# The high and low parts of a Strassen stage's results, queued one unit of products later

## The chip, the cores and the metric

The kernel runs on one core of one Trainium2 chip. A time is device microseconds (us) of one execution of the whole program. A core has four engines that matter here, each of which works through its own queue in the order in which the program issued the instructions: TensorE (PE in the profile, its weight loads PEld), VectorE (DVE), ScalarE (ACT) and GpSimd (POOL, which here mostly issues DMAs). An instruction waits at the head of its queue for what it needs from other engines, and everything behind it waits with it.

## The reference, cut to what matters

One block of a network on x of 2048 rows by 512 columns: a Fourier mixing sublayer, then a gated feed-forward sublayer, each behind a layer norm that is modulated from c. The change touches the second sublayer alone:

```python
gate = jnp.einsum("bsd,df->bsf", x, w1)      # 512 -> 1792
up = jnp.einsum("bsd,df->bsf", x, w3)
h = _silu(gate) * up
out = jnp.einsum("bsf,fd->bsd", h, w2)       # 1792 -> 512
```

## The kernel before, in words

**Numbers in two parts.** TensorE multiplies float32 numbers here as two rounded parts: the high part is a rounded copy (made on ACT, `copy`, line 87), the low part is what the copy left over (made on DVE, `minus`, line 90). `product` (line 100 issues its matmuls) is three matmuls: high by high, high of the left operand by low of the right one, low by high. So a result h that is to be multiplied by w2 needs a tile `hf` with a high and a low half, and the second matmul of its product already reads the low half.

**Tiles.** All large tiles are slots of one pool of 50, taken with `take` from the front of a queue of free slots and put back at its end with `give`. PSUM has eight banks; results leave a bank by a copy on ACT or an addition on DVE.

**Groups.** The 1792 columns of w1 and w3 are 7 groups of 256, and the rows are 4 blocks of 512, two pairs of blocks. From about 318 us on, each item, that is one group with one pair of blocks, is done as a Strassen product: 7 products for w1 (named a1 to a7 below) and 7 for w3 (b1 to b7), where plain blocks need 8. There are 12 items (two groups of the first pair are done as plain blocks before): five of the first pair of blocks (items 0 to 4), then seven of the second (items 5 to 11). Of these, items 5 to 9 (`SEVEN`) also take seven products by w2, and the other items take eight plain ones. A product by w2 is written y; it is read out of its bank on ACT (line 335, tile `y`) and added to DRAM by a DMA that GpSimd issues (line 1160 or 1352).

**Units and queues.** One a, b or y is a unit of six matmuls. The order of units is written by hand as strings. For item i, the units before the dash belong to the item before:

```python
body = "a6 a5 y y a7 y a3 y a4 y b1 y b2 y b6 b5 y"
head = "-b7 a1 -b4 -b3 a2 " if i == turning else "-b7 a1 a2 -b4 -b3 " if i else "a1 a2 "
if i == turning:
    body = "y y y y y a6 y a5 y a7 y b1 b2 a4 b6 a3 b5"
```

So four units of an item's w3 products, b7, b4 and b3 among them, run inside the next item, and the first y that uses an item's results comes after its b3: four units after b4 in the stretches of items 1 to 4, and three after b4 in the stretch of item 5 (`turning`), where five y stand in a row. The items of the second pair use shorter bodies, such as "a6 a5 a7 y a3 a4 y b1 b2 y b6 b5 y".

A unit is issued in this sequence: `delayed()` issues whatever an earlier unit put behind itself for now; then the unit's matmuls, and its reading out of the bank; then `beside` lets a planner issue as many waiting jobs (splitting the next weights, the layer norm of the other rows) as the unit's estimated spare time on DVE and ACT pays for. `behind(n, fn)` puts `fn` n units off, to the head of that unit.

**The results.** `factor` runs one a or b. Of the products of w3, b1, b5 and b6 are only copied out (ACT, line 87, tile `x`); b2, b3 and b7 are added to such a copy (DVE, line 93, tile `x`) and b4 is used from its bank. Then `result` (the function of `times`, line 96, tile `v`) multiplies by the silu of the w1 side, and puts two things behind: the high part, `highs` (ACT, line 87, `hf<-v`), and the low part, `lows` (DVE, line 90, `hf<-v,hf`). For the items of `SEVEN` the results go to `seven_parts`, which does the same for b2, b4 and b7 (`high` and `low`) and a row of sums after b3. Results of b2 and b4 feed the first four y of an item, those of b3 and b7 the next four. After b3, the two tiles `v` are given back, also by `behind`.

In b7 the matmuls add to the bank that b6 began with, so b7 can begin only after b6's copy; a7 stands in the same way to a6. A y needs a free bank of two (6 and 7).

## Time and profile before

| what | before |
|---|---|
| median of 3 executions | 696.4 us (695.23 to 697.4) |
| the profiled execution | 694.86 us |
| its span, first to last instruction | 693.1 us |
| granted TensorE clock, mean | 0.997 |
| PE busy | 675.3 us, 3122 matmuls |
| DVE busy | 586.9 us |
| ACT busy | 451.1 us |
| POOL busy | 131.6 us |

Busy time of PE has to be read with care: a matmul record of 128x512 lasts 389 ns, and in an undisturbed run the next one begins 0.23 us after it, so records overlap and short pauses of PE do not show as idle. A pause is seen in the starts: where two matmuls begin further apart than 0.23 us. In the rows of the timeline, the columns are start, duration, engine, line, operation, out<-in, shape, count, and in brackets the idle time before with what ended it. Equal instructions in a row are merged into one row: two merged matmuls that run undisturbed take 0.61 to 0.63 us.

### The profile page before, as it was taken

How to read it: one execution, taken by the hardware profiler on the slowest of the kernel's cores; microseconds unless marked ns; L12 is line 12 of the kernel's file. 1: busy time of each engine (PE TensorE's matmuls, PEld its weight loads, DVE VectorE, ACT ScalarE, POOL GpSimd, SP SyncE). 2: the span in 40 equal slices, each digit the busy share in tenths (PEclk: the TensorE clock that was granted, in tenths of full speed). 3: DMA queues.
4: the chain of work that ended last, by engine and by line, in shares of the span. 5: the costliest groups of instructions: out<-in, count | busy, mean ns of one | idle time of the engine just before them, and what ended most of it. 6: DMA issues, size and time to landing. Idle time of an engine off the chain costs nothing.

```text
span 693.1 us, 9032 instructions
## 1 busy us (share of the span) xinstructions
PE 675.3 (97%) x3122; PEld 558.1 (81%) x3122; DVE 586.9 (85%) x945; ACT 451.1 (65%) x751; POOL 131.6 (19%) x156
## 2 busy tenths in 40 slices
PE   7999899999999999999999999999999999999996
PEld 5899778888888888888788888887877888888785
DVE  5999759998999988889997989787999979888374
ACT  4998946545353575664577767867676988877520
POOL 1320252543435000010101001011002212221100
PEclk9999999999999999999999999999999999999999
DMA  9730289787588540173667666476849898999713
GB/s 264 222 123 1 71 306 352 259 294 253 181 310 263 181 157 30 37 148 122 102 145 147 152 154 117 96 132 121 258 89 208 152 208 168 186 214 172 179 42 126
DMA packets 40261, 116.80 MB, mean 169 GB/s; under 512 B 5136, under 2 KB 5392, under 8 KB 40208
## 3 DMA queue, kind: packets, MB, share of 16 engines
q0 software_dynamic: 14512, 50.86, 36.5%
q1 hardware_dynamic: 25264, 63.98, 27.9%
q10 hardware_dynamic: 432, 1.31, 0.5%
q8 instruction: 26, 0.43, 0.3%
q14 instruction: 27, 0.22, 0.1%
HBM read 76.81 MB, written 41.42 MB: 171 GB/s over the span
## 4 chain that ended last, share of the span: by engine, by line
PE 71%; DVE 9%; issue 7%; DMA 5%; ACT 4%; POOL 1%; SPq 1%; another core or an unknown queue 1%; POOLq 0%; ACTq 0%; DVEq 0%
PE bank L100 43%; PE bank L750 25%; DMA sum<-y 3%; POOL sum L1352 1%; PE bank L559 1%; DMA w<-in_wdr 1%; PE bank L598 1%; ACT y L335 1%; DVE v L96 1%; SPq L231 1%; DMA w<-in_wdi 1%; DVE xr L805 1%; DVE ul L90 1%; DMA x<-in_x 0%
## 5 line engine op out<-in xcount | busy, mean ns | idle before, releaser
L100 PE MATMUL bank<-hf,w2h 128*128 128x512 f32 (+1 forms) x352 | 108.5, 389 | 0.4 <-ACT y L335 0.4
L87 ACT ACTIVATE hf<-v 128x512 fp32r<-128x512 f32 x71 | 44.4, 631 | 69.1 <-DVE v L96 53.7
L335 ACT ACTIVATE y<-bank,gb 128x512 f32<-128x512 f32 x118 | 76.5, 682 | 4.1 <-PE bank L100 3.6
L100 PEld LDWEIGHTS bank<-hf,w2h 128*128 128x128 f32 x352 | 65.5, 188 | 16.1 <-ACT y L335 2.2
L1160 POOL DMA_DIRECT2D sum<-y x28 | 24.0, 857 | 240.7 <-ACT y L335 124.5
L100 PE MATMUL bank<-hf,w2l 128*128 128x512 f32 (+1 forms) x176 | 68.1, 387 | 0.0
L90 DVE TENSOR_TENSOR hf<-v,hf 128x512 fp32r<-128x512 f32 x71 | 48.7, 686 | 9.8 <-ACT hf L87 9.8
L1352 POOL DMA_DIRECT2D sum<-y x35 | 29.8, 852 | 129.4 <-ACT y L335 120.4
L750 PE MATMUL bank<-d,us 128*128 128x512 f32 x128 | 49.9, 390 | 1.5 <-DVE ho L93 1.5
L87 ACT ACTIVATE x<-bank 128x512 f32<-128x512 f32 x72 | 41.7, 591 | 13.3 <-PE bank L100 12.1
L750 PE MATMUL bank<-bh,us 128*128 128x512 f32 x128 | 49.9, 390 | 0.0
L750 PE MATMUL bank<-bh,ul 128*128 128x512 f32 x128 | 49.8, 389 | 0.0
L750 PE MATMUL bank<-d,uh 128*128 128x512 f32 x128 | 49.8, 389 | 0.0
L750 PE MATMUL bank<-l,us 128*128 128x512 f32 x128 | 49.8, 389 | 0.0
L750 PE MATMUL bank<-l,uh 128*128 128x512 f32 x128 | 49.8, 389 | 0.0
L170 POOL DMA_INDIRECT re<-in_ctr,mirror x32 | 35.1, 1095 | 64.8 <-DVE ul L90 38.5
L170 POOL DMA_INDIRECT im<-in_cti,mirror x32 | 32.9, 1029 | 38.2 <-PE bank L750 10.0
L93 DVE TENSOR_TENSOR x<-bank,x 128x512 f32<-128x512 f32 x36 | 24.7, 685 | 17.3 <-PE bank L100 17.1
L100 PEld LDWEIGHTS bank<-hf,w2l 128*128 128x128 f32 x176 | 33.1, 188 | 6.6
L1244 ACT ACTIVATE v<-v 128x512 f32<-128x512 f32 x36 | 22.7, 629 | 22.5 <-DVE v L93 22.1
L93 DVE TENSOR_TENSOR v<-bank,x 128x512 f32<-128x512 f32 x36 | 24.7, 686 | 13.4 <-PE bank L100 12.5
L100 PE MATMUL bank<-h2h,w1h 128*128 128x512 f32 x80 | 31.1, 389 | 0.0
(260 smaller groups left out, 1904.7 us busy)
## 6 DMA issues: line engine op xcount, KB each, us to landing
sum<-y POOLq DMA_DIRECT2D x63, 512.0 KB
w<-in_w SPq DMA_DIRECT2D x42, 512.0 KB
re<-in_ctr SPq DMA_DIRECT2D x32, 256.0 KB
im<-in_cti SPq DMA_DIRECT2D x32, 256.0 KB
wmc<-in_wmc SPq DMA_DIRECT2D x8, 512.0 KB
xr<-in_xt SPq DMA_DIRECT2D x8, 512.0 KB
sum<-xr SPq DMA_DIRECT2D x8, 512.0 KB
x<-in_x SPq DMA_DIRECT2D x11, 256.0 KB
```

The source lines that it names most:

```text
L87: nc.scalar.activation(dst, src, AF.Copy, scale=scale)
L90: nc.vector.tensor_tensor(out=dst, in0=a, in1=b, op=OP.subtract)
L93: nc.vector.tensor_tensor(out=dst, in0=a, in1=b, op=OP.add)
L96: nc.vector.tensor_tensor(out=dst, in0=a, in1=b, op=OP.mult)
L100: nc.tensor.matmul(acc, lhs[a], rhs[b], start=first and n == 0, stop=last and n == len(PASSES) - 1, skip_group_check=more,)
L170: nc.gpsimd.indirect_dma_start(dst, None, rows, bass.IndirectOffsetOnAxis(ap=at, axis=0))
L231: queue.dma_start(raw_w[dt][q * 64 : (q + 1) * 64, m, :], w[i][par::2, q])
L335: nc.scalar.activation(dst, src, AF.Identity, scale=by)
L750: nc.tensor.matmul(acc[what, e], lhs, rhs, start=begin and i == 0, stop=(end or (turn and what == "x")) and i == len(terms) - 1, skip_grou ...
L1160: nc.gpsimd.dma_start(sums[t, d // 2], y, accum_op=OP.add)
L1244: behind(k != 0 or q == 0, lambda: nc.scalar.activation(v, src, AF.Silu))
L1352: nc.gpsimd.dma_start(sums[t, which], y, accum_op=OP.add)
```

## The change

The high part is put two units behind instead of one, the low part three instead of two, for all items and, in the items of `SEVEN`, for b2, b4 and b7. The tiles `v` of the items outside `SEVEN` are given back four units after b3 instead of three. No instruction is added, removed or resized.

```diff
@@ result
-        behind(1, highs)
-        behind(2, lows)
+        behind(2, highs)
+        behind(3, lows)
@@ seven_parts, if (q, k) != (0, 1)
-            behind(1, lambda: high(n, v[q, k]))
-            behind(2, lambda: low(n, v[q, k]))
+            behind(2, lambda: high(n, v[q, k]))
+            behind(3, lambda: low(n, v[q, k]))
@@ factor, n == 3 of w3
-                    behind(9 if items[i] in SEVEN else 3, lambda x=x: give(x))
+                    behind(9 if items[i] in SEVEN else 4, lambda x=x: give(x))
```

## The prediction

> **What bounds the kernel now.** I read the page first, then what PE waits for after 318 us, then the timeline of PE around every place where two matmuls begin further apart than 0.23 us.

> ```profile
> PE 675.3 (97%) x3122; PEld 558.1 (81%) x3122; DVE 586.9 (85%) x945; ACT 451.1 (65%) x751; POOL 131.6 (19%) x156
> L87 ACT ACTIVATE hf<-v 128x512 fp32r<-128x512 f32 x71 | 44.4, 631 | 69.1 <-DVE v L96 53.7 <-issue 6.7 <-DVE v L90 4.7
> ```
> ```profile
> PE bank L100 <- ACT y L335: 0.9, 2, 0.5
> PE bank L100 <- ACT x L87: 0.6, 2, 0.4
> ```

> TensorE is the bound: 97% busy. The copy that makes the high part (71 of them) leaves ACT idle for 69.1 us, of which 53.7 us are for the multiplication on DVE: ACT stands at the head of its queue with nothing to do, and the readings-out of banks wait behind it. But ACT is not the bound, so those 53.7 us are no prize. What they cost is what reaches PE, and the waits of PE name just two engines' work there, both ACT's: y and x. So the question is narrow: which pauses of PE does a late copy make, and which new pauses does the later place make?

> **The change, part by part: what goes.** In item 0's tail, the copy of b2 waits 3.74 us; y, and the copies of b6 and b5 (one row of two) stand behind it, and b7 begins late.

> ```profile
> 342.61 0.63 ACT L87 ACTIVATE hf<-v 128x512 fp32r<-128x512 f32 x1 [3.74 <-DVE v L96]
> ...
> 343.72 1.07 ACT L87 ACTIVATE x<-bank 128x512 f32<-128x512 f32 x2
> ```
> ```profile
> 343.61 0.39 PE L100 MATMUL bank<-hf,w2l 128*128 128x512 f32 x1
> 344.36 0.50 PE L100 MATMUL bank<-th,w3sh 128*128 128x512 f32 x1 [0.36 <-ACT x L87]
> ```
> ```profile
> 374.18 0.39 PE L100 MATMUL bank<-hf,w2l 128*128 128x512 f32 x1
> 374.50 0.50 PE L100 MATMUL bank<-th,w3sh 128*128 128x512 f32 x1
> 374.84 0.40 PE L100 MATMUL bank<-tl,w3sh 128*128 128x512 f32 x1
> ```

> The matmul of b7 begins 0.75 us after the one before it, 0.52 more than 0.23; and a matmul that has waited takes 0.34 until the next (374.50 to 374.84), 0.11 more than usual. So a pause costs its wait plus 0.11, here 0.63. After the change y stands ahead of the copy of b2, which still begins at 342.61; b6's copy then follows at 343.15, 0.57 earlier, and lands at 343.8, when b7 is due at 343.84: the pause goes, **-0.63**. The pause at 374.50 has the same cause and goes: 0.32 - 0.23 + 0.11, **-0.20**.

> In the stretch of item 11, the copies of b7 and b3 do the same to a y, to the next y and to a7:

> ```profile
> 640.63 0.63 ACT L87 ACTIVATE hf<-v 128x512 fp32r<-128x512 f32 x1 [2.15 <-DVE v L96]
> ...
> 642.30 0.59 ACT L87 ACTIVATE x<-bank 128x512 f32<-128x512 f32 x1
> ...
> 649.75 0.63 ACT L87 ACTIVATE hf<-v 128x512 fp32r<-128x512 f32 x1 [2.26 <-DMA sum<-y]
> ```
> ```profile
> 641.39 0.39 PE L100 MATMUL bank<-h2h,w1l 128*128 128x512 f32 x1
> 641.89 0.74 PE L100 MATMUL bank<-hf,w2sh 128*128 128x512 f32 x2
> ...
> 644.55 0.39 PE L100 MATMUL bank<-th,w3l 128*128 128x512 f32 x1
> 644.91 0.74 PE L100 MATMUL bank<-hf,w2h 128*128 128x512 f32 x2
> ```
> ```profile
> 650.30 0.39 PE L100 MATMUL bank<-th,w1sl 128*128 128x512 f32 x1
> 650.92 0.50 PE L100 MATMUL bank<-th,w1sh 128*128 128x512 f32 x1 [0.23 <-ACT x L87]
> ```

> The three pauses are 0.38, 0.24 and 0.50 us by the same sum. A unit later, b7's copy stands behind the two readings of y, and a1's copy comes a good microsecond before 642.30; b3's copy, which waits for a DMA that still reads its slot, stands behind a6's copy instead of ahead of it. All three go: **-1.12**. Together **-1.95**.

> **What comes.** The low part's place is what I count as the loss. The first y of an item reads the low half of b4's result with its fifth matmul, 0.91 us after its start. Before, DVE has it in queue right behind b3's multiplication. Now it is issued one unit later, so it stands behind the jobs of that unit. In the stretch of item 2 these are the four additions `w3s`:

> ```profile
> 383.54 0.69 DVE L96 TENSOR_TENSOR v<-v,x 128x512 f32<-128x512 f32 x1
> 384.15 0.68 DVE L90 TENSOR_TENSOR hf<-v,hf 128x512 fp32r<-128x512 f32 x1
> 384.75 0.42 DVE L93 TENSOR_TENSOR w3s<-w 128x256 f32<-128x256 f32 x1
> ...
> 386.22 0.69 DVE L90 TENSOR_TENSOR hf<-v,hf 128x512 fp32r<-128x512 f32 x1
> ```
> ```profile
> 384.84 0.63 PE L100 MATMUL bank<-hf,w2h 128*128 128x512 f32 x2
> ```

> The low part at 384.15 lands at 384.83; its reader is the second matmul of the pair that begins at 384.84, due at 385.07: only 0.24 us to spare. The four additions take 386.22 - 384.75 = 1.47 us, begin at 384.15 instead, and the low part begins at 385.62 and lands at 386.31. PE waits 1.30 (with the 0.06 from a landing to the start of its reader), plus 0.11: **+1.41**. Nothing hides it: a late low part holds PE, as the pair of 0.84 us in the next rows shows.

> In the stretches of items 3, 4 and 5 the jobs between differ:

> ```profile
> 412.34 0.69 DVE L96 TENSOR_TENSOR v<-v,x 128x512 f32<-128x512 f32 x1
> ...
> 444.94 1.22 DVE L90 TENSOR_TENSOR w3l<-w,w3h 128x1024 fp32r<-128x1024 f32 x1
> ...
> 472.88 1.22 DVE L90 TENSOR_TENSOR tl<-xc,th 128x1024 fp32r<-128x1024 f32 x1
> ```
> ```profile
> 414.82 0.62 PE L100 MATMUL bank<-hf,w2h 128*128 128x512 f32 x2
> ...
> 444.74 0.84 PE L100 MATMUL bank<-hf,w2h 128*128 128x512 f32 x2
> ...
> 472.18 0.73 PE L100 MATMUL bank<-hf,w2h 128*128 128x512 f32 x2
> ```
> ```profile
> 474.52 0.73 PE L100 MATMUL bank<-hf,w2h 128*128 128x512 f32 x2
> ...
> 477.57 0.74 PE L100 MATMUL bank<-hf,w2h 128*128 128x512 f32 x2
> ```

> Stretch of item 3: the multiplication begins at 412.34, the additions 0.61 later, the low part after 1.47 more, at 414.42, and it lands at 415.10; due is the matmul at 414.82 + 0.23. **+0.24** (0.13 and 0.11). Stretch of item 4: here the additions stand ahead already, and the pair takes 0.84 instead of 0.62, so the low part is late today. It falls behind the weights' low part as well, which holds DVE for 1.13 (1.22 less the overlap of two records): **+1.12**. Stretch of item 5, with one unit less between b4 and y: the low part falls behind the addition of a2 (0.60) and a `tl` (1.13), 1.73 later, and is 0.05 late already (0.73 for the pair): +1.78. Three further pairs of this row of y (the first and the last are shown) pause because ACT has a job for each y and falls behind; while PE waits for the low part, ACT catches up, which gives back up to 0.48. I take **+1.30**, with 1.78 and 0.9 as ends. In the stretch of item 1 no job stands in that unit: nothing.

> In the items of `SEVEN`, the copy of b2 filled the time in which DVE made `w2s`, for which the job behind y, the copy `w2sh`, waits. Now that copy stands first and `hf` behind it, ahead of b6's copy:

> ```profile
> 518.75 0.42 DVE L90 TENSOR_TENSOR w2s<-w,w2s 128x256 f32<-128x256 f32 x1
> ```
> ```profile
> 520.36 0.59 ACT L87 ACTIVATE x<-bank 128x512 f32<-128x512 f32 x1
> ...
> 549.71 0.59 ACT L87 ACTIVATE x<-bank 128x512 f32<-128x512 f32 x1
> ```
> ```profile
> 550.47 0.40 PE L100 MATMUL bank<-th,w3sh 128*128 128x512 f32 x1
> ```

> `w2s` is done at 519.17; `w2sh` then holds ACT for 0.95 and `hf` for 0.54, so b6's copy begins at 520.69 instead of 520.36. b7 waits for that copy there today: **+0.33**. An item later the same shift of 0.33 takes b6's copy from 549.71 to 550.04, landing at 550.63 with b7 due at 550.47: 0.22 and 0.11, **+0.33**. Two further items have by the same sum a few hundredths to spare, and I count nothing for them; 0.2 each is the end.

> **The sum:** +1.41 +0.24 +1.12 +1.30 +0.33 +0.33 -1.95 = **+2.8 us** on a span of 693.1, in an execution of 694.86. That execution lies 1.5 below the median of the three, so I put the sum on the median: 696.4 + 2.8 = **699.2 us**. The tiles `v`, held a unit longer, cost nothing that I can find: it is two slots of 50 for one unit.

> **The rivals.** *The low part stays covered.* If the planner's jobs do not stand between b3's multiplication and the low part (they are paid from a credit, and pauses do not move them, so I doubt it), the loss of 4.07 at the four y goes, and what is left is +0.66 - 1.95: 695.1; without the loss in `SEVEN`, 694.4. That ends on the other side, not slower. It decides at 0.24 us, the slack in the stretch of item 2. Against it speaks the order on DVE: in the stretch of item 4 the additions already stand ahead and PE already pauses.

> *It doesn't reach PE.* ACT's 53.7 us just move to another instruction, b6's copy is as late as before, and lows that come late are absorbed: 696.4. For it speaks that the two waits of PE above are only 1.5 us in all; against it that each pause can be followed to one copy.

> *The clock falls.* The new pauses, of up to 1.9 us, are longer than any after 318 us. The start of the kernel shows what a poorly used PE gets:

> ```profile
> 6.00:9.00 3.00, 1.02 (x3) 0.20 (x2) 2.36 (x7) 0.98 (x2) 0.00 (x0) 1.00 1.02 415
> 9.00:10.00 1.00, 0.98 (x5) 1.00 (x6) 0.22 (x1) 0.89 (x3) 0.00 (x0) 0.61 1.06 406
> 10.00:13.00 3.00, 3.00 (x12) 1.86 (x11) 2.89 (x5) 2.14 (x4) 0.00 (x0) 0.56 1.09 257
> ```

> These windows list the busy time of PE second and the granted clock behind POOL: after 3 us with 1.02 busy the clock was 0.61 and 0.56 for 4 us, a loss of 0.39 + 3 x 0.44 = 1.7 us. One such fall gives 700.9, three give 704.3. [...]

> *A slot waits for a DMA.* The tiles change their slots. One copy waited 2.26 us for a DMA that still read its slot; one such wait ahead of a bank that PE needs gives up to 701.5.

> **How the numbers follow.** Chances: the forecast 0.55 (698.0 to 700.5 by its own ends), the low part covered 0.12, not reaching PE 0.15, the clock 0.08, a slot 0.10. A measurement of this kernel can tell about 0.3%, 2.1 us, from no change: faster is below 694.3, slower above 698.5. Slower gets most of the forecast (0.47) with the clock and the slot, 0.64; faster about half of the covered case, 0.06; the same the rest, 0.30. The range 695.2 to 701.8 leaves out half of the covered case and the upper parts of the last two.

> **What would show it.** In the changed trace, the fifth matmul of the first y should begin late, released by DVE `hf` of line 90: by about 1.3 us in the stretch of item 2, 1.2 in that of item 4, over 1.5 in that of item 5, hardly in that of item 3. The pauses ahead of b7 at 344 and 374, and those at 642, 645 and 651, should be gone; the one near 521 longer. Idle time ahead of `hf<-v` on ACT should fall well below 69.1 us. If the first y of an item shows no pause, the step on the low part is wrong; if the pauses of ACT's making are still there, the first step is.

## The result, and the profile after

The changed kernel takes 698.67 us (median of 13 executions, 697.6 to 701.37) against 695.97 us for the kernel before in the same measurement (695.0 to 697.44). The ratio is 1.0043, with a 95% interval of 1.0034 to 1.0052: slower by 2.4 to 3.6 us, 2.70 by the medians. The forecast was +2.8. The profiled execution took 699.12 us with a granted clock of 0.995.

That agreement is better than the reasons behind it. A good 1.4 us of the loss lie where the prediction looked, between 318 us and the last matmul; at least as much lies behind the last matmul, where it expected nothing. First the page of the changed kernel (columns as in the prediction's rows of the page):

```profile
span 697.3 us, 9017 instructions
...
PE 675.1 (97%) x3122; PEld 558.6 (80%) x3122; DVE 587.2 (84%) x945; ACT 454.3 (65%) x751; POOL 132.9 (19%) x156
...
q14 instruction: 28, 0.23, 0.1%
...
L100 PE MATMUL bank<-hf,w2h 128*128 128x512 f32 (+1 forms) x352 | 108.9, 389 | 2.9 <-DVE hf L90 2.9
...
L87 ACT ACTIVATE hf<-v 128x512 fp32r<-128x512 f32 x71 | 44.2, 628 | 37.9 <-DVE v L96 31.2
```

The view of waits of the changed kernel, PE alone, after 318 us (total, times, longest):

```profile
PE bank L100 <- DVE hf L90: 2.9, 3, 1.6
PE bank L100 <- ACT y L335: 0.5, 1, 0.5
PE bank L100 <- ACT x L87: 0.4, 1, 0.4
```

ACT's idle time ahead of the high part fell from 69.1 to 37.9 us, and PE's waits for ACT from 1.5 to 0.9 us. A wait that did not exist takes their place: 2.9 us for the low part on DVE. These three rows are the prediction's first two steps in small. The timeline of PE in the changed kernel, at the first y of the stretches of items 2, 4 and 5:

```profile
384.72 0.39 PE L100 MATMUL bank<-hf,w2h 128*128 128x512 f32 x1
385.35 0.50 PE L100 MATMUL bank<-hf,w2h 128*128 128x512 f32 x1 [0.24 <-DVE hf L90]
...
445.35 0.39 PE L100 MATMUL bank<-hf,w2h 128*128 128x512 f32 x1
446.82 0.50 PE L100 MATMUL bank<-hf,w2h 128*128 128x512 f32 x1 [1.09 <-DVE hf L90]
...
473.93 0.39 PE L100 MATMUL bank<-hf,w2h 128*128 128x512 f32 x1
475.93 0.50 PE L100 MATMUL bank<-hf,w2h 128*128 128x512 f32 x1 [1.61 <-DVE hf L90]
```

Where the matmuls of a pair began 0.23 to 0.34 us apart, the second one, the fifth of the y, now begins 0.63, 1.48 and 2.00 us after the first.

To compare kernels I add up the pauses: every pair of starts more than 0.30 us apart after 318 us, less 0.227 each. The kernel before has 4.63 us of them, the changed one 6.04: **+1.41**. The second part is the time from the start of the last matmul to the end: 6.68 us before (686.39 to 693.07), 8.94 after (688.40 to 697.34), **+2.26**. The two profiled spans differ by 4.27 us. The 0.6 that are left do not belong to the change: at 318 us, ahead of everything that was changed, the same matmul begins 0.68 us later already.

The view of the two lines of SP's last waits, SP's rows alone (count, duration min/median/max in ns, first and last start), shows where the end grew. SP first takes its branch over a part of the program that is not needed here, then executes eight waits (line 2572) and fourteen more (line 2625). In the kernel before:

```profile
L2625 SPq EVENT_SEMAPHORE  x14: 17/28/28, 691.4 to 693.0; - x14
```

In the changed kernel:

```profile
L2572 SPq EVENT_SEMAPHORE  x8: 17/17/17, 693.4 to 694.0; - x8
...
L2625 SPq EVENT_SEMAPHORE  x14: 17/28/28, 694.1 to 697.3; - x14
```

The same fourteen waits of SP take 1.6 us before and 3.2 us after. One DMA packet of the changed kernel falls into that stretch, by the DMA view from 694.0 to 696.0 us:

```profile
DMA packets 1, 0.01 MB, mean 4 GB/s; under 512 B 0, under 2 KB 0, under 8 KB 0
...
q14 instruction: 1, 0.01, 1.2%
```

It is on the queue that the profile calls instruction, which carries 28 packets in all in the changed kernel (the page above) and 27 in the kernel before. In the trace, the first of the fourteen waits is issued at 694.10 and the second at 695.75: SP sits for 1.65 us at one place in its program, and in the kernel before it does not. The packet is the second of a pair of 8 KB each, which begins at 693.83, 0.43 us after the first of the eight waits. The kernel before has such a pair as well (691.36 and 691.40, 0.52 after the first wait), but twelve of the fourteen waits follow each other there at 0.06 to 0.07 us. The one packet that the kernel before does not have comes behind the gap, at 696.38.

### The profile page after: what moved, and what is told of

Read it like the earlier page. It is cut to its first block, busy times and chain, and to the rows that moved or that the text cites. A ratio compares the mean times of both kernels' runs of the same rounds, so it can differ in the third digit from the quotient of the medians.

```text
span 697.3 us, 9017 instructions
## 1 busy us (share of the span) xinstructions
PE 675.1 (97%) x3122; PEld 558.6 (80%) x3122; DVE 587.2 (84%) x945; ACT 454.3 (65%) x751; POOL 132.9 (19%) x156
## 4 chain that ended last, share of the span: by engine, by line
PE 82%; DVE 8%; ACT 4%; DMA 2%; issue 1%; SPq 1%; another core or an unknown queue 1%; POOL 0%; ACTq 0%; DVEq 0%
PE bank L100 53%; PE bank L750 25%; PE bank L559 2%; DMA w<-in_wdr 1%; PE bank L598 1%; ACT y L335 1%; PE bank L576 1%; DVE x L93 1%; DVE hf L90 1%; SPq L231 1%; DVE v L96 1%; DMA x<-in_x 1%; DMA w<-in_wdi 1%; DVE ul L90 1%
## 5 line engine op out<-in xcount | busy, mean ns | idle before, releaser
L100 PE MATMUL bank<-hf,w2h 128*128 128x512 f32 (+1 forms) x352 | 108.9, 389 | 2.9 <-DVE hf L90 2.9
L335 ACT ACTIVATE y<-bank,gb 128x512 f32<-128x512 f32 x118 | 77.9, 687 | 18.3 <-PE bank L100 14.8
L100 PEld LDWEIGHTS bank<-hf,w2h 128*128 128x128 f32 x352 | 65.6, 188 | 18.8 <-DVE hf L90 4.9
L87 ACT ACTIVATE hf<-v 128x512 fp32r<-128x512 f32 x71 | 44.2, 628 | 37.9 <-DVE v L96 31.2
L100 PE MATMUL bank<-hf,w2l 128*128 128x512 f32 (+1 forms) x176 | 68.1, 387 | 0.0
L87 ACT ACTIVATE x<-bank 128x512 f32<-128x512 f32 x72 | 42.6, 595 | 25.8 <-PE bank L100 23.6
L90 DVE TENSOR_TENSOR hf<-v,hf 128x512 fp32r<-128x512 f32 x71 | 48.6, 684 | 2.0 <-ACT hf L87 2.0
L93 DVE TENSOR_TENSOR x<-bank,x 128x512 f32<-128x512 f32 x36 | 24.7, 685 | 22.5 <-PE bank L100 22.1
L100 PEld LDWEIGHTS bank<-hf,w2l 128*128 128x128 f32 x176 | 33.0, 188 | 6.5
L93 DVE TENSOR_TENSOR v<-bank,x 128x512 f32<-128x512 f32 x36 | 24.8, 688 | 14.3 <-PE bank L100 12.6
L100 PE MATMUL bank<-h2l,w1h 128*128 128x512 f32 x80 | 31.1, 389 | 0.0
```

The costliest lines, as they stand in the source:

```text
L87: nc.scalar.activation(dst, src, AF.Copy, scale=scale)
L90: nc.vector.tensor_tensor(out=dst, in0=a, in1=b, op=OP.subtract)
L93: nc.vector.tensor_tensor(out=dst, in0=a, in1=b, op=OP.add)
L100: nc.tensor.matmul(acc, lhs[a], rhs[b], start=first and n == 0, stop=last and n == len(PASSES) - 1, skip_group_check=more,)
L335: nc.scalar.activation(dst, src, AF.Identity, scale=by)
```

## The experiments

**The theory.** Three causes: the low part of b4, issued a unit later, reaches the first y late (a loss); the high part, issued a unit later, no longer holds up ACT's queue (a gain); and with fewer instructions on SP, a place in its program at which it stands still falls among its last waits (a loss that has nothing to do with the stage). **The rivals:** the two halves do the same harm, or the gain needs both; the end is longer because the last stores come late.

### One copy back: the low part of b4

```diff
-        behind(3, lows)
+        behind(2 if (q, k) == (1, 0) else 3, lows)
...
-            behind(3, lambda: low(n, v[q, k]))
+            behind(2 if n == 2 else 3, lambda: low(n, v[q, k]))
```

> The changed kernel, but the low part of b4's result alone is two units behind again, as before the change; all other parts stay late. Theory (the loss is that one low part, late at the first y of an item): the four pauses of PE inside the first y, 4.2 us in the changed kernel's trace, shrink to under 0.5, the pauses ahead of b7 and y that the change removed stay removed, and the time falls to about 694.2 us, 1.8 below the kernel before. Rival (the stretch of the items only gives 1.4 of the 2.7 us, the rest is an end of the program that the change made longer): it stays at or above the kernel before, 696 to 697.5.

Measured: 694.8 us against 695.55, ratio 0.9991 (0.9979 to 1.0003). PE's waits after 318 us in this kernel:

```profile
PE bank L100 <- ACT y L335: 0.5, 1, 0.5
PE bank L100 <- ACT x L87: 0.4, 1, 0.4
```

The row with DVE is gone, and the pauses fall from 6.04 to 2.59 us. So the late low part of b4 is worth 3.45 us of pauses, and everything else that the change moves is a gain of 2.04 in them against the kernel before. The time, forecast at 694.2, is not clear of the kernel before: the end takes the gain back, it is 8.67 us here, too.

### The highs alone, the lows alone

For the first, the changed kernel with the low parts and the return of the tiles as before; for the second, with the high parts alone as before; the same in `seven_parts` for both:

```diff
 highs alone
-        behind(3, lows)
+        behind(2, lows)
...
 lows alone
-        behind(2, highs)
+        behind(1, highs)
```

> Only the high parts are put a unit later (two behind); the low parts are two behind as before, so high and low are issued at the head of the same unit, and v is given back as before. Theory (the copy's later place gives, the low part's later place costs): pauses at 344, 374 and 642 to 651 us gone, no pause of over 0.4 us inside a first y, the pauses ahead of b7 at 521 and 551 of the SEVEN items longer by 0.3 each: 694.2 us, 1.8 below the kernel before. Rival (it is the copy's later place on ACT that costs): at least 1 us above the kernel before.

> Only the low parts are put a unit later (three behind), and v is given back as in the changed kernel; the high parts are one behind as before. Theory: the new pauses at the four first y, about 4.1 us by the prediction's steps, come without the 1.95 that the copies gave: 699.5 to 700 us, some 1 us above the changed kernel. Rival (copies cost, or the end of the program does): no slower than the changed kernel, 696 to 698.7.

Measured: the highs alone 696.14 us, ratio 1.0007 (0.9992 to 1.0022), pauses 3.53 us; a gain of 1.10 us in the pauses, and the longer end (8.73 us) takes it away. The lows alone 703.21 us, ratio 1.0100 (1.0080 to 1.0119), pauses 12.74 us, far more than was expected. The halves do not add: -1.10 and +8.11 would give +7.0 instead of +1.41. Of these missing 5.6 us, 3.4 lie in the stretch of item 2. The timelines of DVE and PE with the lows alone show what happens there:

```profile
376.18 1.22 DVE L90 TENSOR_TENSOR w2l<-w,w2h 128x1024 fp32r<-128x1024 f32 x1 [2.28 <-ACT w2h L87]
...
383.15 0.69 DVE L93 TENSOR_TENSOR v<-bank,x 128x512 f32<-128x512 f32 x1 [1.54 <-ACT x L87]
...
388.88 0.68 DVE L90 TENSOR_TENSOR hf<-v,hf 128x512 fp32r<-128x512 f32 x1
```
```profile
387.19 0.39 PE L100 MATMUL bank<-hf,w2h 128*128 128x512 f32 x1
389.62 0.50 PE L100 MATMUL bank<-hf,w2h 128*128 128x512 f32 x1 [2.04 <-DVE hf L90]
```

With the high part of b2 at the head of ACT's queue, the copy `w2h` behind it comes late. The low part of b2, a unit later, no longer stands ahead of `w2l` on DVE, so DVE waits 2.28 us for `w2h`, and further on 1.54 for the copy `x`: 3.82 us of waits between the multiplications of b2 and b3, where the kernel before has 2.59 and the changed one 1.61. All that DVE has queued, the low part of b4 last, is later for it. After that pause the clock fell, and 1.6 of the 12.74 us are matmuls that began 0.43 us apart for that reason. The same kernel by windows (PE's busy time second, the granted clock behind POOL):

```profile
384.00:387.00 3.00, 3.00 (x15) 2.48 (x14) 2.96 (x5) 1.80 (x4) 0.00 (x0) 1.00 0.83 277
387.00:390.00 3.00, 0.96 (x5) 0.49 (x4) 2.96 (x7) 3.00 (x5) 0.00 (x0) 1.00 0.51 209
390.00:394.00 4.00, 4.00 (x13) 3.18 (x12) 3.04 (x4) 1.65 (x3) 0.79 (x1) 0.63 0.00 0
394.00:400.00 6.00, 6.00 (x27) 4.87 (x27) 4.50 (x9) 3.94 (x6) 0.26 (x2) 0.96 0.50 89
```

2.04 us of waiting were followed by 4 us at a clock of 0.63, with 13 matmuls in 4 us where one each 0.227 us makes 17 to 18. This is the prediction's rival of the clock, and in the profiled execution of this kernel, the slowest of its five, it came true; the pause of the changed kernel in the same place is 0.63 us from start to start, and the clock stayed whole. Here a lower clock followed a wait of 2.04 us once, and none followed the 1.61 us of the changed kernel near 474 (granted clock 1.00 from 318 to 690 us). At which length of a pause the clock falls, no run shows.

### One kind of item alone

The changed kernel with the items of `SEVEN` as before, and the changed kernel with the plain items and the return of their tiles as before:

```diff
 plain items alone, in seven_parts
-            behind(2, lambda: high(n, v[q, k]))
-            behind(3, lambda: low(n, v[q, k]))
+            behind(1, lambda: high(n, v[q, k]))
+            behind(2, lambda: low(n, v[q, k]))
...
 items of SEVEN alone, in result and factor
-        behind(2, highs)
-        behind(3, lows)
+        behind(1, highs)
+        behind(2, lows)
-                    behind(9 if items[i] in SEVEN else 4, lambda x=x: give(x))
+                    behind(9 if items[i] in SEVEN else 3, lambda x=x: give(x))
```

> The change in the items outside SEVEN alone; b2, b4 and b7 of the SEVEN items have their old places. Theory: the pauses at the four first y stay, those ahead of b7 at 521 and 551 us lose the 0.3 each that the change added, and the pause near 536 us may come back (0.65), so 698 to 699 us, as the changed kernel within 0.7. Rival (the loss sits in the SEVEN items): under 697.

> The change in the three copied results of the groups with seven products alone; the plain groups and the return of their tiles as before. By the theory of the prediction's two terms: the pauses near 521 and 551 grow by 0.3 each (0.4 to 0.7 and 0.1 to 0.4) with the copy of b2's high part behind the copy of w2's high part; the pauses near 349, 374, 386, 415, 447 and 476 and at 642, 645 and 651 as in the kernel before or, where the low part of b4 in these groups sets them, gone in the last stretch (642, 645, 651: 1.1 us less). Sum of the pauses 4.0 to 5.3 us against 4.63, time 0.6 below to 0.7 us above the kernel before plus whatever the end after the last matmul gains. Rival (the plain groups' change set those two pauses as well): 521 and 551 as in the kernel before.

Measured: the plain items alone 697.49 us, ratio 1.0038 (1.0022 to 1.0054), pauses 5.79 us; those near 384, 414, 445 and 473 are there, those near 344, 374, 642, 645 and 651 are gone, and the ones near 521 and 551 have about their old size (0.38 instead of 0.42, and nothing). The items of `SEVEN` alone 697.43 us, ratio 1.0046 (1.0033 to 1.0059), pauses 4.87 us: near 521 and 551 they are 0.71 and 0.34, and all others of the kernel before stay but one; two of 0.11, near 509 and 623, are new. The profiled execution of this kernel had a clock of 0.989, so its places are compared, not its span. So each of the prediction's terms belongs to the kind of item that it named.

The one that went was not on the prediction's list. In the plain items alone it is still there (timeline of PE):

```profile
538.00 0.39 PE L100 MATMUL bank<-th,w1sl 128*128 128x512 f32 x1
538.79 0.73 PE L100 MATMUL bank<-hf,w2h 128*128 128x512 f32 x2 [0.40 <-ACT y L335]
```

With the items of `SEVEN` alone, it isn't (timeline of PE, the same two units):

```profile
538.35 0.39 PE L100 MATMUL bank<-th,w1sl 128*128 128x512 f32 x1
538.58 0.65 PE L100 MATMUL bank<-hf,w2h 128*128 128x512 f32 x2
```

0.79 from start to start becomes 0.23. The pause of 0.65 us near 536 in the kernel before is a bank that waits for the reading of a y; the late copies in the items of `SEVEN` bring that reading forward. It takes both halves: the highs alone leave 0.56 of it; with the low part of b4 back 0.11 is left, and 0.54 in the better version below, where the high part of b2 is back as well.

### Where SP's last instructions lie

To test the end by itself, instructions are added to SP's program that are never run: `drain` instructions of SP in the general branch, which SP jumps over in every execution. Ten of them in the changed kernel put as many SP instructions ahead of the last stretch as the kernel before has (590, against 580, counted in the program as built); 246 of them in the kernel before make 836, 256 more than in the changed kernel. That the gap comes back 256 instructions later was the author's assumption until this run.

```diff
@@ general
     nc.sync.dma_start(cc, cp)
+    for _ in range(10):
+        nc.sync.drain()
```

> The changed kernel with ten SP drain instructions added in the general branch, which is jumped over in every run: nothing that is executed differs, only where SP's last instructions lie in its program (590 SP instructions ahead of them, as in the kernel before, instead of 580). Theory A (part of the change's cost is a fetch of instructions by SP in the row of its last waits, 1.63 us in the changed kernel's profile, that the kernel before doesn't have): the time from the last matmul to the end is 6.7 to 6.9 us instead of 8.94, no gap of over 1 us among SP's last waits, 27 instruction packets on queue q14, and a median 1.4 to 2.0 us below the changed kernel's 698.7, so 696.7 to 697.3; the pauses of TensorE are those of the changed kernel, 6.0 us in sum. Theory B (the longer end is the last stores or their landing, set by the moved copies): 8.7 to 9.0 us after the last matmul, median 698.4 to 699.

> The kernel before with 246 SP drain instructions added in the general branch, jumped over in every run. 836 SP instructions then stand ahead of SP's last ones, which is 256 more than in the changed kernel, so that with blocks of 128 or of 256 instructions its end lies in a block as the changed kernel's does. Theory A (fetch of instructions in SP's last waits): the end after the last matmul grows from 6.68 to 8.2 to 9.0 us with a gap of 1.4 to 1.9 us among SP's last waits and one more packet on q14, and the median is 1.4 to 2.0 us above the kernel before, ratio 1.002 to 1.003, without any change in TensorE's pauses (4.6 us). Theory B (the end depends on the moved copies): no gap, 6.7 us after the last matmul, ratio 1.000.

Measured: the changed kernel with ten more 695.52 us, ratio 1.0019 (1.0006 to 1.0033), where the changed kernel had 1.0043: 0.24% or 1.7 us less (0.6 to 2.8 by the two intervals), with the same pauses (6.03 us) and an end of 7.04 us, a little above the 6.9 that was expected at most. The kernel before with 246 more 695.96 us, ratio 1.0034 (1.0021 to 1.0048), with the same pauses as before (4.63 us) and an end of 8.48 us. The rival of the late stores is ruled out for this part: no store was moved. SP's last fourteen waits and the instruction queue, in the changed kernel with ten more, by the view of the line (2627 with the two lines added) and by the page:

```profile
L2627 SPq EVENT_SEMAPHORE  x14: 17/28/28, 692.9 to 694.5; - x14
```
```profile
q14 instruction: 27, 0.22, 0.1%
```

The same of the kernel before with 246 more:

```profile
L2627 SPq EVENT_SEMAPHORE  x14: 17/28/28, 690.6 to 693.8; - x14
```
```profile
q14 instruction: 28, 0.23, 0.1%
```

1.6 us against 3.2 us, with 27 and 28 packets. Over all kernels the gap stands behind the same instruction, when the eight waits and the fourteen are counted through: 580 ahead and a gap behind the ninth wait (the changed kernel), 581 and the eighth (the low part of b4 back), 583 and the sixth (highs alone), 578 and the eleventh (plain items alone), 588 and the first (items of `SEVEN` alone), each time the 589th; with 589 (lows alone) and 590 there is no gap, and 836 has it behind the ninth, as 580 has: the 845th, 256 further on. The later the gap comes, the shorter it is by and large, from 2.22 us behind the first wait to 1.39 behind the eleventh: in all six kernels that have one, the wait behind it is issued 2.2 to 2.4 us after the first wait. All ten kernels begin the pair of packets 0.1 to 0.5 us after the first wait, and SP stands still only where the 589th or the 845th instruction lies among the last waits.

### The better version

The low part of b4 back in every item, the high part of b2 back in the items of `SEVEN`, and nine unused SP instructions, which make 590:

```diff
-        behind(3, lows)
+        behind(2 if (q, k) == (1, 0) else 3, lows)
...
-            behind(2, lambda: high(n, v[q, k]))
-            behind(3, lambda: low(n, v[q, k]))
+            behind(1 if n == 1 else 2, lambda: high(n, v[q, k]))
+            behind(2 if n == 2 else 3, lambda: low(n, v[q, k]))
...
+    for _ in range(9):
+        nc.sync.drain()
```

> The changed kernel with two copies back at their old place: the low part of b4 in every group (one unit earlier) and the high part of b2 in the groups with seven products (one unit earlier), and nine SP drain instructions in the general branch, jumped over, so that 590 SP instructions stand ahead of SP's last ones. Theory: the low part of b4 cost 3.5 us of pauses, SEVEN's b2 0.3 to 0.7, the end 1.4 to 2.0; everything else that the change moves is a gain. Pauses 1.9 to 2.3 us in sum against 4.63 of the kernel before, 6.7 to 6.9 us after the last matmul: 692.6 to 693.6, ratio 0.9955 to 0.997. Rival (the end isn't set by where SP's instructions lie, and b2 is not what the two pauses wait for): 694.4 to 695, ratio 0.998 to 0.9995.

Measured: 691.79 us against 693.86 of the kernel before on the same chip, ratio 0.9965 (0.9952 to 0.9978). It is faster than both kernels, the one before by 2.1 us. PE's pauses are 2.39 us, 0.1 above what was expected at most. The timeline of PE:

```profile
520.50 0.39 PE L100 MATMUL bank<-hf,w2l 128*128 128x512 f32 x1
521.00 0.50 PE L100 MATMUL bank<-th,w3sh 128*128 128x512 f32 x1
...
535.88 0.39 PE L100 MATMUL bank<-th,w1sl 128*128 128x512 f32 x1
536.54 0.73 PE L100 MATMUL bank<-hf,w2h 128*128 128x512 f32 x2 [0.27 <-ACT y L335]
```

With b2's copy back, the pause near 521 is small again and the one near 536 is back. Taking back b2 gains 0.20 us over the kernel with the low part of b4 back (2.59 to 2.39), not the 0.66 that the prediction charged it with; most of this version's advantage over that one is the end, 7.12 us instead of 8.67.

### All of it side by side

The second to fourth columns are differences against the profile of the kernel before, in us; their sum is set against the ratio that was measured, times 696.

| kernel | pauses | end | sum | by the ratio |
|---|---|---|---|---|
| changed | +1.41 | +2.26 | +3.7 | +2.4 to +3.6 |
| low part of b4 back | -2.04 | +1.99 | -0.1 | -1.5 to +0.2 |
| highs alone | -1.10 | +2.05 | +1.0 | -0.6 to +1.5 |
| lows alone | +8.11 | +0.13 | +8.2 | +5.6 to +8.3 |
| plain items alone | +1.16 | +1.51 | +2.7 | +1.5 to +3.8 |
| items of `SEVEN` alone | +0.24 | +2.14 | +2.4 | +2.3 to +4.1 |
| changed, ten more | +1.40 | +0.36 | +1.8 | +0.4 to +2.3 |
| before, 246 more | 0.00 | +1.80 | +1.8 | +1.5 to +3.3 |
| better version | -2.24 | +0.44 | -1.8 | -3.3 to -1.5 |

Pauses and end together account for all nine, the changed kernel 0.1 above the end of its interval.

## Why the prediction was right, and where it was not

**The total was right by two errors that cancel,** which is luck. +2.8 was forecast and +2.7 measured. Of the pauses the forecast had 1.4 too much; of the end it knew nothing, and that is some 1.7 us by the experiment (2.26 in the profiles).

**The pauses that go: right.** Those at 344, 374, 642, 645 and 651 are gone, -1.95 as forecast, and they belong to the plain items. That they come from the high part is shown by the highs alone, where all five are gone.

**The low part of b4, item by item:** forecast +0.24, +1.12 and +1.30 in the stretches of items 3, 4 and 5; measured +0.22, +1.13 and +1.28 (2.00 - 0.23 and 0.11 for the matmul behind it, less the 0.60 of pauses that were there). The kernel with that low part back shows the cause.

**The stretch of item 2: the mechanism right, the size wrong.** +1.41 was forecast, +0.51 measured (0.63 - 0.23 and 0.11). The step that failed took the multiplication of b3 to begin at 383.54 as before, and put only the four additions ahead of the low part. What changed its start is the high part of b2, some 12 us earlier. The timeline of ACT in the kernel before, then in the changed kernel:

```profile
371.81 0.63 ACT L87 ACTIVATE hf<-v 128x512 fp32r<-128x512 f32 x1 [2.52 <-DVE v L96]
...
372.92 1.05 ACT L87 ACTIVATE w2h<-w 128x1024 fp32r<-128x1024 f32 x1
```
```profile
371.29 1.05 ACT L87 ACTIVATE w2h<-w 128x1024 fp32r<-128x1024 f32 x1
372.24 0.62 ACT L87 ACTIVATE hf<-v 128x512 fp32r<-128x512 f32 x1
```

And the timeline of DVE, in the same order:

```profile
372.47 0.69 DVE L90 TENSOR_TENSOR hf<-v,hf 128x512 fp32r<-128x512 f32 x1 [0.70 <-ACT hf L87]
374.00 1.23 DVE L90 TENSOR_TENSOR w2l<-w,w2h 128x1024 fp32r<-128x1024 f32 x1 [0.83 <-ACT w2h L87]
...
383.54 0.69 DVE L96 TENSOR_TENSOR v<-v,x 128x512 f32<-128x512 f32 x1
```
```profile
372.37 1.23 DVE L90 TENSOR_TENSOR w2l<-w,w2h 128x1024 fp32r<-128x1024 f32 x1 [0.54 <-ACT w2h L87]
373.51 0.69 DVE L90 TENSOR_TENSOR hf<-v,hf 128x512 fp32r<-128x512 f32 x1
...
382.53 0.69 DVE L96 TENSOR_TENSOR v<-v,x 128x512 f32<-128x512 f32 x1
...
384.61 0.69 DVE L90 TENSOR_TENSOR hf<-v,hf 128x512 fp32r<-128x512 f32 x1
```

Before, the high part of b2 waits at the head of ACT's queue, the copy `w2h` stands behind it, and DVE waits for both: 0.70 us for the low part of b2, then 0.83 for `w2l`. With both halves later, `w2h` runs 1.63 us earlier, `w2l` goes first, and DVE waits 0.54 in all. So b3's multiplication begins 1.01 us earlier while PE is 0.12 earlier. The additions still stand between (382.53 to 384.61), but from an earlier start: 1.41 - 0.89 = 0.52. From the multiplication of b2 to that of b3 DVE takes 11.4 us in the five kernels in which both halves of b2 are late in the plain items, 12.5 in the three in which both have their old place, 12.3 with the highs alone and 13.6 with the lows alone. The prediction followed the high part to PE, and not to DVE's own waits for ACT.

**The items of `SEVEN`: right in place, incomplete.** +0.33 and +0.33 were forecast near 521 and 551; measured +0.27 and +0.37. The pause of 0.65 near 536, on no list, went with both halves in their later place. Two pauses of 0.11 each are new (near 509 and 624), and the one near 514 grew by 0.02. So the sum of the pauses: 0.51 + 0.22 + 1.13 + 1.28 + 0.27 + 0.37 + 0.24 - 1.95 - 0.65 = 1.42.

**The rivals.** That the low part stays covered is refuted by PE's 2.9 us of waits for it; that the change does not reach PE, by the pauses that came and went. The clock did not fall in the stage of the changed kernel (1.00 from 318 to 690 us); the 0.08 that the forecast gave it was the author's estimate. No slot waited long enough to show in PE's waits.

**What was missed altogether** is the end. The forecast counted what the change adds and removes as nothing but order. That no instruction is added or removed is true of the work, and not of the waits: another order needs other waits. SP executes five wait instructions fewer in the changed kernel, 161 against 166 (and its general branch has five fewer), and so the 589th instruction, behind which SP stands still for 1.65 us, falls among the last waits. Nothing in the prediction looks behind the last matmul.

**Still open.** With ten more instructions the changed kernel's end is still 0.36 us longer than before. In its trace the issue of the last store but one takes 0.93 us instead of 0.36 in the kernel before (1.05 in the changed kernel, 0.36 in the plain items alone). What sets this was not tried. Nor was it tried whether the gap goes when SP's last waits themselves are fewer.

## What to carry to other kernels

When a split copy is moved in an in-order queue, follow both halves and what stands behind each of them on its own engine: a high part that is moved later lets the copies behind it go first (here `w2h`, by 1.63 us), and with them whatever waits for these copies on another engine, and a low part that is moved later pays for all the jobs that slip in ahead, until its first reader, which is the second matmul of its product. Move each by the distance to its own reader: here one of the low parts was worth 3.45 us of pauses, and with it back the others' move was a gain of 2.04 us of pauses. And before a difference of 0.3% is put down to the part that was edited, compare the time from the last matmul to the end, and look for a gap among SP's last waits.
